# A new instruction list, and one accumulator moved, in the head of a fused state-space and feed-forward kernel

## The chip, the cores and the metric

The kernel runs on one core of a Trainium2 chip. The metric is the device time of one execution in microseconds (us). A core has a matrix engine (TensorE, PE in the profile; its weight loads are PEld), a vector engine (VectorE, DVE), a scalar engine (ScalarE, ACT), a general engine (GpSimd, POOL) and a fifth (SyncE, SP) that here only issues transfers. Each engine runs its own instructions strictly in the order in which they were written; engines wait for each other by semaphores. PE writes its results to PSUM, eight banks of 512 fp32 numbers per partition.

## The reference

Two layers. The first is a chunked state-space recurrence over 4 batches, 8 heads, 768 rows; the second is a feed-forward layer with a squared ReLU over the 3072 rows of 256 numbers that come out.

```python
log_a = np.log(np.clip(a, 1e-06, 1.0))
for c in range(nc):                                  # chunks of 32 rows
    cum = np.cumsum(la, axis=-1)
    L = np.exp(cum[:, :, :, None] - cum[:, :, None, :]) * causal
    M = np.einsum('bhin,bhjn->bhij', Cc, Bc) * L
    y_intra = np.einsum('bhij,bhjd->bhid', M, xc)
    y_inter = np.einsum('bhin,bhnd->bhid', Cc, state) * decay_to_i[:, :, :, None]
    y[:, :, sl] = y_intra + y_inter
    state = decay_full * state + np.sum(Bx, axis=2)  # Bx = B x, decayed to the chunk's end
...
h = np.maximum(x @ w_in, 0.0)
return h * h @ w_out
```

x has 32 numbers per head and row, B and C 16; w_in is 256 x 2048, w_out 2048 x 256.

## The kernel before

**Units and blocks.** The work is cut into 12 units of 256 rows of one batch with all 8 heads; unit k is batch k % 4 and third k // 4 of the rows. In the names, units and blocks count from 0, so "unit one" has the names that end in 0 (xs0, mts0, T0) and "unit two" those that end in 1. A unit's rows lie two to a partition (r = 0, 1), and its partitions in two halves of 64 (i = 0, 1), which are its two chunks: chunk 0 starts from the state before, chunk 1 from chunk 0's.

**The decay.** Instead of the decays between pairs of rows, the kernel uses the running product P of `a` within a chunk: C is multiplied by P and x by 1/P. `ac` clamps `a` (L538), `sk` is the scan that makes the running product (L470), `sp` and `p` bring it to rows on partitions by fp32 matmuls against an identity (`prep_p`, L454) and form chunk totals (L528, L549); copies out of PSUM make P_sb and Ptot (`ps`, `to`; `p` also copies), `iv` takes reciprocals (Pinv, L558), `fq` and `pq` make Pquad. The first 64 rows of `a` serve units 0 to 3 (`fa`, `ac0`, `sk0`, PSUM bank 4), the other 128 rows all later units (`la`, `ac1`, `sk1`, `pp1`, `p2`).

**A unit's steps**, in the order of its data: load B, C, x (`ldB`, `ldC`, `ldx`); C P and B to bf16 side by side in jt (`pc` L159, `pb` L167 and L171), x / P in xs (`px` L179); transposes on PE (`tr` L197, for unit 0 in the parts `trC` and `trB`) and their copies to bct (`tc`, `tcC`, `tcB`, L210 and L212); scores into banks 0 to 3, one for each pair of heads (`mt` L222); the causal mask, either directly (`mk`, DVE, L231) or by a score copy on ACT (`sc` L236) and a product on POOL or DVE (`ms` L240); state sums B'x (`u`, 16 matmuls, helper line L247); intra products (`in`; `ina` and `inb` are the halves that use the first and last two masks), the carry from the state (`ca`); copies T of the result (`t`, L210, L212, L284) and us of the state sums (`us`, L298). Sd is the state spread over four heads' blocks (`sf` straight from PSUM on DVE, L345; later `z`, L317 and L322, and `s` on POOL, L333). u, the intra products and the carry of a unit share a pair of banks; each engine's access to a bank waits for another engine's earlier one, whichever columns they use.

**The feed-forward layer.** Block k is unit k's 256 rows. For each of 8 groups f of 256 hidden features, `a0` to `l7` are the first layer's four matmuls of 256 columns (L405, bank by bank), with the ReLU on ACT into hb (L410); `qa0` and so on is the square on DVE (L416); `A0` to `L7` are the second layer's four matmuls (L432, accumulated in bank 6 or 7). The weights come in four loads each, issued by POOL (`wi` L140, `wo` L144).

**The order.** The kernel schedules by hand: the string ORDER lists every step, and each engine gets its instructions in the order of the list. A suffix `:a`, `:v`, `:p`, `:s` names the engine (ACT, DVE, POOL, SP). `id12:128` is twelve filler matmuls of 128 columns on constants (L477), which compute nothing that is used and keep PE running. `gB3` and `afC2` hold back the loads that follow by a small write or read on POOL.

Of the kernel before, what the change touches and what calls it, by code (L numbers as in the profile page):

```python
# [30 lines left out]
def kernel(  # L31
# [13 lines left out]
    nc = tc.nc  # L45
# [3 lines left out]
        fa1:a jz0:v ef jz1:p id12:128 ti fa0:s la0:s id15:128 pi eb ldB0:s ac0:v ldC0:a sk0 ku sp la1:a pbh0:p hd  # L49
        id1:256 pc0:v pbl0:v mb:a id7:128 trC0 ps iv:8:16 tcC0:1:a tcC0:0:v trB0 la2:s tcB0:2:v pk id4:128 iv1:0:8  # L50
        id2:256 ldx0:s mt0 wi0 la3:s px0:v ldC1:s ac1:p su id8:128 ldB1:s wi1 ldx1:s u0:67 mk0 mk0 mk0 pc1:p sc0
        pb1:a tr1 to id5:256 tc1:1:a tc1:0:v jz2:a ms0:p sk1 fq sf0 wo0 wi2 px1:p mt1 ina0 inb0 ca0 mk1 mk1 t0:aa
        sc1 us0 pp1:a mk1 a0 ldC2:s a1 u1 ina1 ms1:v pc2 inb1 p2 sf1 ca1 t1:va us1 a3 qa1 ldB2:s qa0 wo1 wi3 a2
        wo2 b0 qa3 qb0 b1 qb1 fr b2 b3 A0 A1 B0 pb2:p B1 tr2 zb0 qb3 b4 a4 iv:32:64 zb1 tc2:1:v qa2 tc2:0:v b5 sb1
        sb0 qb4 ldx2:s a5 qb2 qa4 mt2 gB3 sc2 ldB3:s ldC3:s B3 iv:16:32 px2 mk2 sc2 A3 ms2:v A2 mk2 qa5 a6 b6
        ms2:p B2 a7 qb5 pb3:a qa6 b7 A5 u2 ina2 ldx3:s inb2 sf2 wo3 pc3 px3 ld4 A4 tr3 ca2 tc3:1:v t2:aa B4 us2 B5
        tc3:0:v u3:45 pc4 mt3 us3 sc3 c5 qb7 qb6 mk3 za3 pb4 ld5 c3 qa7 c4 qc5 c0 tr4 qc3 px4 pb5 sa3 c1 c6 ld6
        qc4 pc5 tr5 qc0 A6 px5 pq A7 wm c2 B6 c7 C0 ms3:v mk3 qc6 mk3 qc7 afC2 pc6 pb6 B7 C3 C6 C4 qc1 bk rg4 C1
        qc2 d1 d0 za4 sa4 mk4 mk4 d3 mk4 C5 d4 qd0 d2 mk4 px6 C2 C7 ld7 zb4 qd1 sb4 qd2 qd3 zb3 rg5 sb3 D0 tr6 mk5
        za5 zb5 sa5 sb5 D1 iv:64:96 mk5 d5 qd4 D2 pb7 d6 qd5 d7 qd6 D3 zb2 e0 qd7 mk5 e1 qe0 sb2 D4 mk5 D5 ld8 pc7  # L60
        e2 qe1 D6 e3 qe2 px7 D7 rg6 e4 qe3 za6 sa6 tr7 zb6 mk6 e5 qe4 sb6 e6 qe5 e7 qe6 mk6 E0 E1 E2 E3 ld9 px8
        mk6 f0 qe7 E4 f1 qf0 pc8 E5 pb8 E6 mk6 f2 qf1 f3 qf2 E7 rg7 mk7 F0 f4 qf3 za7 tr8 F1 F2 f5 qf4 f6 qf5 f7
# [713 lines left out]
```

## Time and profile before

| what | us |
|---|---|
| median of 3 runs | 117.34 |
| the 3 runs | 117.34, 117.55, 115.72 |
| the profiled execution, its own time | 116.09 |
| its span, first to last instruction | 114.4 |
| mean granted clock of PE | 0.985 |
| PE, ACT, DVE, POOL busy | 108.4, 77.4, 84.4, 52.2 |

The rows that are shown below come from four views of that execution. A row of the timeline has the start in us, the busy time in us, the engine, the line of the kernel, the operation, output <- inputs, the shapes, how many were merged (x), and in brackets how long the engine was idle before it and what ended that. A row of the chain of waits has start, duration and what the chain went through. A row of the windows has the stretch, its length, the busy time and number of instructions of an engine, PE's granted clock, the share of the DMA engines and GB/s. A row of DMA issues has what is loaded, the queue, the size and the median time from issue to landing. Durations of PE overlap, as matmuls are pipelined.

### The profile page before, as it was taken

The page shows a single profiled execution, that of the slowest core. Times are in us where ns is not written, and L with a number is a line of the kernel's source. Part 1 is how long each engine was busy: PE and PEld are TensorE (multiplying, and loading weights), DVE is VectorE, ACT ScalarE, POOL GpSimd, SP SyncE. Part 2 cuts the span into 40 slices and gives each one's busy share as a digit, 9 for nine tenths or more (in the row PEclk, how much of TensorE's full clock was granted, in tenths as well). Part 3 has the DMA queues.
Part 4 walks back from the last instruction along what each step waited for, and adds up shares of the span by engine and source line. Part 5 has one row for each costly group of instructions (what it writes and reads, how often), then busy time and mean ns, then how long its engine had stood idle before and what let it go on. Part 6 is the DMA issues. An engine that isn't in the chain of part 4 may idle for free.

```text
span 114.4 us, 4062 instructions
## 1 busy us (share of the span) xinstructions
PE 108.4 (95%) x1658; PEld 96.5 (84%) x1658; DVE 84.4 (74%) x185; ACT 77.4 (68%) x158; POOL 52.2 (46%) x98
## 2 busy tenths in 40 slices
PE   7967899999999999999999999999999999999990
PEld 7845499898898889989989989989889899899980
DVE  2697566998899799989965989659578388345430
ACT  1744777677794785686587687786777776966840
POOL 7699950499298946659402769047020020000000
PEclk9999599999999999999999999999999999999999
DMA  2999999099998908988628538350051020020202
GB/s 40 198 196 193 217 196 188 10 183 169 189 163 140 317 10 181 215 192 164 131 80 158 112 113 149 87 145 19 6 141 22 6 95 0 14 83 0 92 6 92
DMA packets 47827, 13.47 MB, mean 118 GB/s; under 512 B 44288, under 2 KB 45888, under 8 KB 47808
## 3 DMA queue, kind: packets, MB, share of 16 engines
q1 hardware_dynamic: 44864, 10.88, 45.9%
q0 software_dynamic: 1664, 2.10, 11.4%
q10 hardware_dynamic: 1280, 0.23, 1.0%
q8 instruction: 13, 0.21, 0.7%
q14 instruction: 6, 0.05, 0.1%
HBM read 10.58 MB, written 3.15 MB: 120 GB/s over the span
## 4 chain that ended last, share of the span: by engine, by line
PE 87%; POOL 3%; DMA 3%; SPq 2%; issue 1%; ACT 1%; DVE 0%; ACTq 0%
PE pp L405 38%; PE pp L432 37%; PE pp L247 7%; PE pp L222 3%; DMA a_nat<-in_a_dram 3%; POOL mts L240 1%; SPq L565 1%; SPq L126 1%; POOL jt L159 1%; POOL w_in_b L140 1%; PE pp L197 1%; ACT T L210 1%; DVE Sd L345 0%; POOL a_cl L538 0%; SPq L116 0%
## 5 line engine op out<-in xcount | busy, mean ns | idle before, releaser
L410 ACT ACTIVATE hb<-pp 128x512 bf16<-128x512 f32 x96 | 54.6, 603 | 22.5 <-PE pp L405 21.4
L416 DVE TENSOR_TENSOR h<-hb 128x512 bf16<-128x512 bf16 x96 | 46.0, 498 | 12.1 <-ACT hb L410 11.8
L405 PE MATMUL pp<-T,w_in_b 128*128 128x256 bf16 x384 | 54.2, 276 | 0.5 <-ACT T L210 0.5
L432 PE MATMUL pp<-w_out_b,h 128*128 128x256 bf16 (+1 forms) x400 | 53.8, 268 | 0.0
L405 PEld LDWEIGHTS <-w_in_b 128*128 128x128 bf16 x384 | 41.8, 114 | 3.1 <-issue 1.8
L432 PEld LDWEIGHTS <-h 128*128 128x128 bf16 x400 | 37.7, 98 | 4.3 <-issue 0.6
L231 DVE TENSOR_TENSOR mts<-pp,mask 128x512 bf16<-128x512 f32 x43 | 28.5, 678 | 0.9 <-PE pp L222 0.9
L333 POOL TENSOR_TENSOR Sd<-z,Pquad 128x256 bf16<-128x256 f32 x16 | 10.6, 666 | 33.9 <-DVE z L317 24.0
L179 POOL TENSOR_TENSOR xs<-x_nat,Pinv 128x256 bf16<-128x256 f32 (+1 forms) x19 | 14.7, 788 | 3.8 <-DMA x_nat<-in_x_dram 2.4
L159 POOL TENSOR_TENSOR jt<-C_nat,P_sb 128x128 bf16<-128x128 f32 x22 | 9.5, 451 | 0.0
L317 DVE SCALAR_TENSOR_TENSOR z<-z,Ptot,us 128x64 f32<-128x64 f32 x8 | 2.4, 296 | 6.6 <-ACT us L301 5.5
L439 ACT COPY osb<-pp 128x512 f32<-128x512 f32 x11 | 6.4, 583 | 0.4 <-PE pp L432 0.4
L247 PE MATMUL pp<-mts,xs 64*32 64x128 bf16 x384 | 6.1, 226 | 0.5 <-DVE Sd L345 0.5
L477 PE MATMUL pp<-const-bfloat16-1.0 128*128 128x128 bf16 (+1 forms) x54 | 5.7, 275 | 0.8 <-PEq L760 0.8
L477 PEld LDWEIGHTS <-const-bfloat16-1.0 128*128 128x128 bf16 x54 | 4.6, 124 | 0.9 <-issue 0.8
L284 ACT CAST T<-pp 128x512 bf16<-128x512 f32 x7 | 4.1, 586 | 1.8 <-PE pp L247 1.5
L247 PEld LDWEIGHTS <-xs 64*32 64x32 bf16 x384 | 4.4, 94 | 0.8 <-issue 0.7
L222 PE MATMUL pp<-bct 32*64 32x256 bf16 x192 | 5.1, 280 | 0.0
L167 POOL CAST jt<-B_nat 128x256 bf16<-128x256 f32 x9 | 4.3, 473 | 1.1 <-DMA B_nat<-in_B_dram 1.1
L247 PE MATMUL pp<-bct,Sd 128*128 128x128 bf16 x40 | 4.3, 223 | 0.0
L210 ACT CAST T<-pp 128x256 bf16<-128x256 f32 x9 | 3.1, 376 | 1.5 <-PE pp L247 1.2
L197 PE MATMUL pp<-eye_b,jt 128*128 128x128 bf16 x24 | 2.5, 221 | 1.2 <-ACT Ptot L531 0.7
(67 smaller groups left out, 57.6 us busy)
## 6 DMA issues: line engine op xcount, KB each, us to landing
x_nat<-in_x_dram SPq DMA_DIRECT2D x12, 256.0 KB, 4.0
out_dram<-osb SPq DMA_DIRECT2D x11, 256.0 KB, 2.2
B_nat<-in_B_dram SPq DMA_DIRECT2D x12, 128.0 KB, 3.2
C_nat<-in_C_dram SPq DMA_DIRECT2D x11, 128.0 KB, 3.3
w_in_b<-in_moe_w_in_dram POOLq DMA_DIRECT2D x4, 256.0 KB, 5.9
w_out_b<-in_moe_w_out_dram POOLq DMA_DIRECT2D x4, 256.0 KB, 5.1
C_nat<-in_C_dram ACTq DMA_DIRECT2D x1, 128.0 KB, 2.5
bct<-jt SPq DMA_TRANSPOSE x8, 2.9
```

The lines of the kernel that those rows point to most:

```text
L159: eng.tensor_tensor(out=_fap(jt[k % 3], 128 + 144 * g, [[384, 2], [32, 4], [1, 16]]), in0=_fap(loaded[k]["C"], 128 * g, [[16, 2], [32, 4], ...
L179: eng.tensor_tensor(out=_fap(xs, 256 * r, [[256, 2 // n], [32, 8], [1, 32]]), in0=_fap(loaded[k]["x"], 32 * r, [[32, 2 // n], [64, 8], [1, ...
L222: nc.tensor.matmul(pp[64 * u:64 * u + 64, q, r * 256:r * 256 + 256], bct[32 * q:32 * q + 32, r, 0, u * 64:u * 64 + 64], _fap(bct[32 * q:32 ...
L231: nc.vector.tensor_tensor(out=live[k]["mts"][:, q].rearrange("p r g i -> p (r g i)"), in0=pp[:, q, :], in1=mask, op=ALU.mult)
L247: nc.tensor.matmul(dst, w, v, start=bool(need), stop=False, skip_group_check=True, **({} if pos is None else {"tile_position": pos}))
L333: nc.gpsimd.tensor_tensor(out=_fap(S_d, 0, [[128, 2], [32, 4], [1, 32]]), in0=_fap(z, 0, [[32, 2], [0, 4], [1, 32]]), in1=_fap(Pquad, 4 * ...
L405: nc.tensor.matmul(pp[:, h, i * 256:(i + 1) * 256], _fap(w, g * w.shape[2] + (o // 2) * 512 + 2 * (o % 2) + i, [[4, 128]]), T[blk][:, g].r ...
L410: nc.scalar.activation(out=hb.rearrange("p i t -> p (i t)"), in_=pp[:, h, :], func=AF.Relu)
L416: nc.vector.tensor_tensor(out=h2, in0=hb, in1=hb, op=ALU.mult)
L432: nc.tensor.matmul(dst, h2[:, i, r * 128:(r + 1) * 128], w_out_b[gi][:, 2 * o + i, c0:c1], start=first, stop=(fp == 7 and i == 1), skip_gr ...
L439: nc.scalar.copy(out=osb, in_=pp[:, 6 if blk == 1 else 7, :])
L477: nc.tensor.matmul(pp[:, h, 0:int(cols)], ones_b[:, 0:128], ones_b[:, 0:int(cols)] if dep is None else dep, start=True, stop=True, skip_gr ...
```

## The change

The head of ORDER is listed anew, up to the first steps of block 3; from `tr6` on the list is the same. Three definitions change with it. `u1:4` puts the state sums of chunk 0 of unit two (k = 1) into bank 4, columns 256 to 319, instead of the bank that its intra products use; us1 and Sd read them there. `p2` now only runs the fp32 products of the late rows of `a`, and its bank stays taken; the copies of Ptot and P_sb are the new step `pd2`. The mask copy moves from ACT to DVE (`mb:v`), the zeroing of jt0 from DVE to ACT and of jt2 from ACT to DVE (`jz0:a`, `jz2:v`), the first half of unit 0's B from DVE to POOL (`pbl0:p`), the second B copy of bct from DVE to ACT. On POOL the first weight issue (`wi0`) now stands ahead of the two B copies; on DVE the scan of the late rows (`sk1`) stands ahead of xs0 and of unit 0's masks; on ACT `pp1` and `ps` stand between the copies of bct0 and the score copy. On SP x of unit 0 is issued after the last two loads of `a` instead of between them. `ina0` and `inb0` come ahead of `mt1`, `tr2` and `mt2` ahead of the first `a4`. The fillers are 66 instead of 54.

```diff
     ORDER = """
-        fa1:a jz0:v ef jz1:p id12:128 ti fa0:s la0:s id15:128 pi eb ldB0:s ac0:v ldC0:a sk0 ku sp la1:a pbh0:p hd
-        id1:256 pc0:v pbl0:v mb:a id7:128 trC0 ps iv:8:16 tcC0:1:a tcC0:0:v trB0 la2:s tcB0:2:v pk id4:128 iv1:0:8
-        id2:256 ldx0:s mt0 wi0 la3:s px0:v ldC1:s ac1:p su id8:128 ldB1:s wi1 ldx1:s u0:67 mk0 mk0 mk0 pc1:p sc0
-        pb1:a tr1 to id5:256 tc1:1:a tc1:0:v jz2:a ms0:p sk1 fq sf0 wo0 wi2 px1:p mt1 ina0 inb0 ca0 mk1 mk1 t0:aa
-        sc1 us0 pp1:a mk1 a0 ldC2:s a1 u1 ina1 ms1:v pc2 inb1 p2 sf1 ca1 t1:va us1 a3 qa1 ldB2:s qa0 wo1 wi3 a2
-        wo2 b0 qa3 qb0 b1 qb1 fr b2 b3 A0 A1 B0 pb2:p B1 tr2 zb0 qb3 b4 a4 iv:32:64 zb1 tc2:1:v qa2 tc2:0:v b5 sb1
-        sb0 qb4 ldx2:s a5 qb2 qa4 mt2 gB3 sc2 ldB3:s ldC3:s B3 iv:16:32 px2 mk2 sc2 A3 ms2:v A2 mk2 qa5 a6 b6
...
+        fa0:s ku fa1:a ac0:v ldC0:a ef sk0 la1:a hd ti jz0:a pi jz1:p id25:128 la0:s pk jz2:v mb:v ldB0:s eb sp
+        iv1:0:8 wm pc0:v wi0 la2:s pbl0:p id1:512 pbh0:p id6:128 la3:s trC0 tcC0:0:a trB0 ac1:p tcB0:2:a ldx0:s
+        tcC0:1:v sk1 ldC1:s id6:128 ldB1:s mt0 pp1:a px0:v mk0 mk0 ps su u0:67 mk0 id8:128 sc0 id3:256 to pb1:a
+        ldx1:s id3:128 wi1 pc1:p tr1 ina0 ms0:p fq tc1:1:v inb0 ldC2:s iv:8:16 ldB2:s wo0 sf0 tc1:0:a px1:p wi2
+        mt1 mk1 mk1 id4:128 ca0 mk1 wo1 id1:128 t0:aa sc1 id9:128 us0 a0 ms1:v a1 u1:4 p2 ina1 sf1 inb1 zb0 ca1
+        t1:aa qa0 us1 wi3 pc2 a2 pd2 qa2 a3 qa3 qa1 pb2:a b0 ldx2:s b1 fr b3 b2 qb0 tr2 tc2:0:v tc2:1:v A0 A1 qb1
+        B0 qb3 iv:16:32 mt2 wo2 qb2 mk2 px2 pq gB3 B1 a5 a4 b4 ldB3:s sb0 b5 mk2 mk2 ldC3:s B3 qa4 A3 zb1 B2 mk2
...
-    def ph_u(k, h, begun):
+    def ph_u(k, h, begun, own=False):
         v, last = live[k], UNITS[k][1] == 2
         v["h"] = h
+        v["uat"] = [(4, 128 * (k + 1)) if own and i == 0 else (h[i], 256) for i in range(2)]
         for r in range(2):
             for i in range(2 - last):
                 for q in range(4):
-                    mm(begun, i, [q], pp[32 * q:32 * q + 32, h[i], 256:320],
+                    at, c = v["uat"][i]
+                    mm(set() if r == 0 and own and i == 0 else {(0, q)} if own and i == 0 else begun, i, [q], pp[32 * q:32 * q + 32, at, c:c + 64],
...
             nc.tensor.matmul(pp[:, h, 128:144], spread, pick_p[1], start=True, stop=True, skip_group_check=True)
+            busy.add(h)
+            second["h"] = h
+
+        second = {}
+
+        def second_out():
+            h = second["h"]
+            busy.discard(h)
             A.copy(out=Ptot[:, 8:24], in_=pp[:, h, 128:144])
             A.copy(out=P_sb[:, :, 32:96], in_=_fap(pp, h * 512, [[64, 2], [1, 64]]))
...
         def first_u(k, hs=None):
             v = live[k]
-            v["h"] = tuple(int(c) for c in hs) if hs else pair()
+            own = hs == "4"
+            v["h"] = ((6, 7) if k == 0 else pair()) if own else tuple(int(c) for c in hs) if hs else pair()
```

More of the change, by code (lines that the diff above doesn't have):

```diff
@@ L295, in ph_uc @@
         us = spool.tile([128, 2, 64], FP32, tag="us", name=f"us{k}", bufs=8)
-        h = v["h"]
-        if h[1] == h[0] + 1 and not last:
-            nc.scalar.copy(out=us, in_=_fap(pp, h[0] * 512 + 256, [[512, 2], [1, 64]]))
+        at = [512 * h + c for h, c in v["uat"]]
+        if not last and (at[1] - at[0] == 512 or v["uat"][0][0] == 4 and v["uat"][0][1] != 256):
+            nc.scalar.copy(out=us, in_=_fap(pp, at[0], [[at[1] - at[0], 2], [1, 64]]))
         else:
             for i in range(2 - last):
-                nc.scalar.copy(out=us[:, i], in_=pp[:, h[i], 256:320])
+                nc.scalar.copy(out=us[:, i], in_=_fap(pp, at[i], [[1, 64]]))
         v["us"] = us
```

36 lines of the change are left out of this document (18 added, 18 removed).

## The prediction

> **What bounds the kernel now.** I read the page first, then the chain of waits from the start to 45 us, then the timeline of the first 20 us engine by engine, and the busy time and clock in windows of 3.41 us, the length of the stretch at half clock.
>
> ```profile
> span 114.4 us, 4062 instructions
> ...
> PE 108.4 (95%) x1658; PEld 96.5 (84%) x1658; DVE 84.4 (74%) x185; ACT 77.4 (68%) x158; POOL 52.2 (46%) x98
> ...
> PEclk9999599999999999999999999999999999999999
> ```
>
> PE is busy for 95% of the span, so the end is fixed by two things: the matmuls that must be run, and the time at which PE gets into the dense stream of feed-forward matmuls. The fifth slice shows a clock of one half. The chain shows what stands before the stream:
>
> ```profile
> 3.26 2.92 DMA a_nat<-in_a_dram
> ...
> 6.27 0.41 POOL a_cl L538
> ...
> 7.37 0.73 POOL w_in_b L140
> ...
> 8.94 1.10 POOL mts L240
> 10.05 0.33 POOL Pquad L534
> ...
> 10.40 0.43 DVE Sd L345
> ...
> 11.67 0.64 ACT T L210 x2
> ...
> 12.35 1.87 PE pp L405 x8
> 14.22 0.60 PE pp L247 x42
> ...
> 15.66 2.66 PE pp L405 x24
> ...
> 29.27 0.28 ACT us L298
> ```
>
> The last load of `a` releases POOL; POOL's queue (clamp, a weight issue, C of unit two, the mask product, Pquad) releases the first state Sd, the carry, the copies of T, and then a0 and a1, the first eight feed-forward matmuls, at 12.35. From 15.66 the chain is PE without a break, but for the copy of us3 at 29.27. A later start of this stream is paid in full.
>
> ```profile
> 4.10:7.51 3.41, 3.28 (x70) 1.00 1.00 193
> 7.51:10.92 3.41, 1.88 (x31) 1.00 1.21 201
> 10.92:14.33 3.41, 2.94 (x62) 0.50 1.17 211
> ```
>
> Columns: window, its length, PE busy and matmuls, granted clock, DMA share, GB/s. After a window in which PE was busy 1.88 of 3.41 us (55%), the next has half the clock; after one of 86% it is whole again. So a0 and a1 took 1.87 us, against 8/24 of 2.66, 0.89, later.
>
> **The head, step by step.** The list moves most of the first 150 instructions, so I place the new order with the durations of the old one.
>
> ```profile
> 4.00 0.19 POOL L481 TENSOR_SCALAR_AFFINE_SELECT quad<-quad 128x4 f32<-128x4 f32 x1
> 4.71 0.29 POOL L171 CAST jt<-B_nat 128x128 bf16<-128x128 f32 x1 [0.52 <-DVE jt L159]
> 4.97 0.21 ACT L700 COPY P_sb<-pp 128x64 f32<-128x64 f32 x1 [0.70 <-DVE jt L159]
> 5.22 0.25 DVE L558 RECIPROCAL Pinv<-P_sb 128x16 f32<-128x16 f32 x1
> 5.26 0.93 POOL L140 DMA_DIRECT2D w_in_b<-in_moe_w_in_dram  x1 [0.26 <-issue]
> 5.89 0.42 PE L222 MATMUL pp<-bct 32*64 32x256 bf16 x16
> 6.12 0.69 DVE L179 TENSOR_TENSOR xs<-x_nat,Pinv 128x512 bf16<-128x512 f32 x1
> 6.27 1.04 POOL L538 TENSOR_SCALAR a_cl<-a_nat 128x128 f32<-128x128 f32 x1
> 6.46 0.59 ACT L236 CAST sc<-pp 128x512 bf16<-128x512 f32 x1 [0.38 <-PE pp L222]
> 6.73 1.88 DVE L231 TENSOR_TENSOR mts<-pp,mask 128x512 bf16<-128x512 f32 x3
> 8.18 0.77 POOL L159 TENSOR_TENSOR jt<-C_nat,P_sb 128x128 bf16<-128x128 f32 x2
> 9.34 0.36 DVE L212 COPY bct<-pp 128x384 bf16<-128x384 bf16 x1 [0.73 <-PE pp L197]
> 9.61 0.73 DVE L470 TENSOR_TENSOR_SCAN cp<-a_cl,const-float32-0.0 128x128 f32<-128x128 f32 x1
> 12.82 0.34 ACT L542 ACTIVATE pick_p<-pick,cp 128x16 f32<-128x16 f32 x1
> ```
>
> POOL's constants end at 4.19 in either order. Then the first weight issue now stands ahead of the B copies: 4.19 + 0.26 + 0.93 = 5.38; two B copies of 0.29, one of them DVE's before, end at 5.96. The last load of `a` is issued one place earlier, as x of unit one now follows it; at the old 2.92 us it lands about 5.7. So the clamp starts at 5.97 instead of 6.27. Its length is uncertain: the chain gives it 0.41, the timeline 1.04. I carry both ends: 6.38 or 7.01.
>
> The scores of unit one come later: from the old B copy's end (5.00) to the scores (5.89) were 0.89 us, so 6.85 now, over by 7.27. This costs nothing by itself, since the scan of the late rows stands ahead of x and of the masks on DVE, and waits for the clamp. Queued behind that wait on DVE are xs0, three mask products and the copy for unit two's scores; PE (u0, the intra products, mt1) waits for these. Scan 0.73: 7.16 or 7.79 with 0.05 for the hand-over. xs0 0.69: 7.87 or 8.5, against 6.81 before. Masks 1.88: 9.77 or 10.4, against 8.61. Copy of bct1 0.36, reciprocal 0.25, Sd 0.43: 10.85 or 11.5. DVE replaces POOL as what ends last: the other feeder runs pick_p 0.34, P_sb 0.21 and score copy 0.59 on ACT to 8.35 or 9.0, C of unit two 0.77 and mask 1.10 and Pquad 0.33 on POOL to 10.0 or 10.65, and is early.
>
> What the change gains here is behind Sd. Before, Sd's end (10.83) to a0 (12.35) took 1.52 us, with all the intra products and both copies of T inside. Now the intra products run in halves before it, and only the carry (some 0.3) and two overlapped T copies, half of the 0.64 being exposed, remain: I take 0.85, for a0 at 11.7 or 12.35, a gain of 0.65 or nothing. The fillers are under these waits and cost nothing: PE has nothing else there.
>
> **From a0 to the dense stream.** Here two things go.
>
> ```profile
> 12.82 0.52 DVE L240 TENSOR_TENSOR mts<-sc,mask 128x512 bf16<-128x512 bf16 x1 [0.20 <-ACT sc L236]
> 14.85 0.42 DVE L345 TENSOR_TENSOR Sd<-pp,Pquad 128x256 bf16<-128x256 f32 x1 [1.50 <-PE pp L247]
> 7.57 0.41 ACT L167 CAST jt<-B_nat 128x256 bf16<-128x256 f32 x1 [0.53 <-DMA B_nat<-in_B_dram]
> 16.22 3.09 ACT L410 ACTIVATE hb<-pp 128x512 bf16<-128x512 f32 x6
> 20.00:25.00 5.00, 4.90 (x12) 1.00 0.42 71
> ```
>
> Sd of unit two waited 1.50 us for PE, because the intra products wrote the bank that holds its sums; with the sums in bank 4 it waits for u1 alone. And if PE keeps its whole clock, a0 and a1 take 0.89. PE's side: a0 + 0.89 + (15.66 - 14.22 =) 1.44 gives 14.0 or 14.7. DVE's side: Sd + masks 1.88 + 0.52 + Sd 0.42 + the carry gives 14.0 or 14.65. They agree: the stream starts 1.66 or 0.96 us earlier than 15.66. I take the middle, 1.3, as nothing tells the two clamp lengths apart. The fp32 products are on PE either way; their copies, moved behind an eviction, cost ACT the same and are 0.3 us of cover.
>
> Some of it is given back. ACT has, behind the T copies (about 14.5), us1, Ptot and P_sb, B of unit three (0.41) and evictions at 3.09/6 = 0.515 each; tr2, now ahead of the first second-layer products, waits for that B copy until about 16.95, where PE would arrive at 14.0 + 2.66 = 16.66. And DVE, busy 4.90 us of the 5 from 20 to 25 (last row), has the squares and the masks of unit three in the same stretch; a wait for a mask can take some 0.5. Bounds: zero if DVE catches up as it did, 1.0 if both are paid. I take 0.4, below the middle, since the shift also moves DVE's inputs forward. The us3 copy (0.28 and hand-overs) is now behind B5: 0.3 gained.
>
> The weights are no bound:
>
> ```profile
> w_in_b<-in_moe_w_in_dram POOLq DMA_DIRECT2D x4, 256.0 KB, 5.9
> ```
>
> The first lands about 4.5 + 5.9 = 10.4, before 11.7. The rest, after 30 us, has the same instructions in the same order.
>
> **Sum.** -1.3 + 0.4 - 0.3 = -1.2: a span of 113.2. The profiled execution's own time was 116.09 for 114.4, so 1.69 more: 114.9; rounding kept, 114.84, I say 114.8. Own range: 116.09 - 1.66 - 0.3 = 114.1 to 116.09 - 0.96 + 1.0 - 0.3 = 115.8. The profiled time is 1.25 below the median of the three runs (117.34, from 115.72 to 117.55); if that scatter is the clock's, it goes with it. Two per cent of 117.34, about what a measurement of this kernel can tell from no change, is 2.35: the marks are 114.99 and 119.69.
>
> Two rules beside the rows. First, the clock: the 55% window is the row above, and its longest wait of PE is this one, 0.65:
>
> ```profile
> 8.03 0.23 PE L197 MATMUL pp<-eye_b,jt 128*128 128x128 bf16 x1 [0.65 <-ACT Ptot L531]
> ```
>
> The Trainium skill (TensorE: Matmul & The Clock Gate, Why this matters for your kernels) asks only for no idle gap of over about 3 us; by that rule neither kernel would lose its clock, and the clock term of this sum would be zero, but this trace disagrees: the clock fell after waits of 0.65 at most. Second, the scan: 0.73 us on 128 rows stood beside POOL's mask product. The Trainium skill (GPSIMD Engine Reference, 1. Specifications) says that GpSimd shares its SBUF interfaces with VectorE and contends with instructions of two SBUF inputs; by it the scan, now beside a weight issue, could be shorter, which no row here separates from the larger tile.
>
> **Rivals.**
>
> *The clock falls all the same.* Between 7.27 and xs0 (7.87 or 8.5) PE is idle, 0.36 or 0.99 us of the window that ends at 10.92, so at most 89% or 71% busy, where 55% lost the clock and 86% kept it. If lost, the stretch from a0 to 14.33 runs at half: 2.0 to 2.6 us lose 1.0 to 1.3, ACT is no longer late, and 0.3 stays: 116.09 - 1.3 + 1.15 - 0.3 = 115.6.
>
> *ACT and DVE take it all.* The dense stream starts early and is held at tr2, mt2 and the masks of unit three, with DVE at 98% there: 116.09 - 0.96 + 1.0 = 116.1, the 0.3 of us3 swallowed too: no change.
>
> *The scan holds DVE for a late load.* Speaks for it: DVE's queue stands behind one small load, and the first weight transfer now starts before that load must land.
>
> ```profile
> C_nat<-in_C_dram SPq DMA_DIRECT2D x1, 128.0 KB, 5.8
> ```
>
> This C load, issued at 5.93 beside the first weights, took 5.8 us. If the `a` load of 2.79 is slowed as much, it lands at 8.6, 2.6 after the clamp's place. All behind it moves by 2.6 from the late end (a0 at 14.95), and PE, idle till 11, loses its clock for one whole window, half of 3.41: 1.7. With 0.7 given back and the 0.3 of us3: 116.09 - 0.96 + 2.6 + 1.7 + 0.7 - 0.3 = 119.8. It is slower than the median from a slip of about 0.1 us with that window lost, and over the mark from 2.5. Against it: 16 KB, and issued before the weights.
>
> **Chances.** Forecast 0.56, of which 0.40 lies under 114.99; clock falls 0.20; ACT and DVE take it 0.10; the scan held 0.14. So faster 0.40, same 0.46, slower 0.14. The range goes from 113.6 (both low ends, and 0.5 for steps priced too long) to 118.0 (the clock's case, on the scatter of 1.25 above, and a slip below 1).
>
> **What would show it.** In the profile of the changed kernel: the clamp at about 6 and the scan right behind it; xs0 ending at 7.9 to 8.5 and the masks at 9.8 to 10.4; a0 at 11.7 to 12.35; Sd of unit two with no wait for intra products; no half in the clock line after 10 us; 24 feed-forward matmuls from 14.0 to 14.7. Wrong if the scan waits past 7.1, if a half clock stands after 11 us, or if PE has breaks of over 1 us between 16 and 24.

## The result, and the profile after

The changed kernel took 118.88 us in the median of 4 runs (117.76 to 119.50), the kernel before, beside it, 117.08 us (115.72 to 117.55). The ratio is 1.0282, with a 95% interval from 1.0215 to 1.0349: slower, where 114.8 was forecast. This ratio, like those below, is of fast runs alone, those within 1.5% of the fastest of their kernel; the two medians would give 1.015.

| | before | after |
|---|---|---|
| profiled execution, its own time, us | 116.09 | 119.50 |
| its span, us | 114.4 | 117.8 |
| mean granted clock of PE | 0.985 | 0.971 |
| first weight issue on POOL, start, us | 5.26 | 4.43 |
| B of unit two: copy on ACT, start, us | 7.57 | 11.19 |
| stream of 24 feed-forward matmuls, start, us | 15.50 | 18.77 |

(The 15.66 of the prediction is the same start in the chain of waits, which counts a matmul from the end of the one before; from here on I use the timeline's.) The page of the changed kernel:

```profile
span 117.8 us, 4074 instructions
...
PE 110.3 (94%) x1670; PEld 98.0 (83%) x1670; DVE 81.5 (69%) x185; ACT 76.2 (65%) x157; POOL 50.1 (43%) x98
...
PEclk9998559999999999999999999999999999999999
```

DVE, ACT and POOL have less to do than before. The clock line has a half in two slices, the fifth and the sixth, instead of in the fifth alone. The chain of waits of the changed kernel says what came first:

```profile
4.38 6.73 DMA B_nat<-in_B_dram
...
11.19 0.41 ACT jt L167
...
11.65 0.82 PE pp L197 x6
...
15.47 1.71 PE pp L407 x8
...
18.93 2.62 PE pp L407 x24
```

Before, the chain went from a load of `a` through POOL to the first state. Now it goes from SP's load of B of unit two, which takes 6.73 us to land, over its copy on ACT, to the transposes of unit two on PE. That load was issued at 4.35 before, 0.03 us earlier, and landed in 3.2 us, so that its copy started at 7.57. The timelines of POOL, DVE, ACT and PE give the rest of the head:

```profile
4.43 0.93 POOL L140 DMA_DIRECT2D w_in_b<-in_moe_w_in_dram  x1
6.00 0.65 POOL L540 TENSOR_SCALAR a_cl<-a_nat 128x128 f32<-128x128 f32 x1
...
6.68 0.42 DVE L472 TENSOR_TENSOR_SCAN cp<-a_cl,const-float32-0.0 128x128 f32<-128x128 f32 x1 [0.94 <-POOL a_cl L540]
7.02 0.67 DVE L179 TENSOR_TENSOR xs<-x_nat,Pinv 128x512 bf16<-128x512 f32 x1
7.61 1.88 DVE L231 TENSOR_TENSOR mts<-pp,mask 128x512 bf16<-128x512 f32 x3
...
11.19 0.41 ACT L167 CAST jt<-B_nat 128x256 bf16<-128x256 f32 x1 [3.00 <-DMA B_nat<-in_B_dram]
...
11.65 0.82 PE L197 MATMUL pp<-eye_b,jt 128*128 128x128 bf16 x6 [2.39 <-ACT jt L167]
...
18.77 2.78 PE L407 MATMUL pp<-T,w_in_b 128*128 128x256 bf16 x24
```

Clamp, scan, scaled x and masks of unit one run as forecast or a little earlier (masks done at 9.49). Then ACT stands 3.00 us for the load and PE 2.39 us for ACT, and intra products, scores and everything else are queued behind these transposes. The windows of the changed kernel show what the gap does to the clock:

```profile
7.51:10.92 3.41, 1.65 (x32) 1.00 1.13 186
10.92:14.33 3.41, 2.68 (x62) 0.51 1.21 198
14.33:17.74 3.41, 3.41 (x43) 0.50 0.87 141
```

PE was busy 1.65 us of 3.41 (48%) in the first of these, and in the next two it had half its clock. The first of those two was itself busy for only 79%, at half clock.

### The profile page after: what moved, and what is told of

It reads as the page before. It is cut to its first block, busy times and chain, and to the rows that moved or that the text cites. A ratio compares the mean times of both kernels' runs of the same rounds, so it can differ in the third digit from the quotient of the medians.

```text
span 117.8 us, 4074 instructions
## 1 busy us (share of the span) xinstructions
PE 110.3 (94%) x1670; PEld 98.0 (83%) x1670; DVE 81.5 (69%) x185; ACT 76.2 (65%) x157; POOL 50.1 (43%) x98
## 4 chain that ended last, share of the span: by engine, by line
PE 87%; DMA 6%; SPq 3%; POOL 1%; ACT 1%; issue 1%; ACTq 0%
PE pp L407 37%; PE pp L434 35%; PE pp L247 7%; DMA B_nat<-in_B_dram 6%; PE pp L222 4%; PE pp L479 1%; SPq L126 1%; SPq L575 1%; PE pp L197 1%; POOL xs L179 1%; PE pp L456 0%; ACT jt L167 0%; SPq L116 0%; PE pp L551 0%; ACT osl L745 0%
## 5 line engine op out<-in xcount | busy, mean ns | idle before, releaser
L412 ACT ACTIVATE hb<-pp 128x512 bf16<-128x512 f32 x96 | 55.3, 604 | 24.2 <-PE pp L407 22.1
L418 DVE TENSOR_TENSOR h<-hb 128x512 bf16<-128x512 bf16 x96 | 44.0, 477 | 13.2 <-ACT hb L412 13.0
L231 DVE TENSOR_TENSOR mts<-pp,mask 128x512 bf16<-128x512 f32 x45 | 29.8, 680 | 1.2 <-PE pp L222 1.2
L479 PE MATMUL pp<-const-bfloat16-1.0 128*128 128x128 bf16 (+1 forms) x66 | 7.1, 279 | 0.8 <-PEq L771 0.8
L479 PEld LDWEIGHTS <-const-bfloat16-1.0 128*128 128x128 bf16 x66 | 5.8, 126 | 1.5 <-issue 1.2
L212 DVE COPY bct<-pp 128x384 bf16<-128x384 bf16 (+1 forms) x5 | 1.6, 341 | 4.9 <-PE pp L197 4.9
L197 PEld LDWEIGHTS <-jt 128*128 128x128 bf16 x24 | 1.8, 107 | 3.5 <-ACT jt L167 2.6
```

The source lines that it names most:

```text
L231: nc.vector.tensor_tensor(out=live[k]["mts"][:, q].rearrange("p r g i -> p (r g i)"), in0=pp[:, q, :], in1=mask, op=ALU.mult)
L412: nc.scalar.activation(out=hb.rearrange("p i t -> p (i t)"), in_=pp[:, h, :], func=AF.Relu)
L418: nc.vector.tensor_tensor(out=h2, in0=hb, in1=hb, op=ALU.mult)
L479: nc.tensor.matmul(pp[:, h, 0:int(cols)], ones_b[:, 0:128], ones_b[:, 0:int(cols)] if dep is None else dep, start=True, stop=True, skip_gr ...
```

## The experiments

Medians below stand beside the kernel before on the same chip: 115.50 us for e1 to e4 (19 runs), 115.50 for e5 to e7 (14), 115.23 for e8 to e10 (19), 115.29 for e11 and e12 (1), 116.75 for e13 to e16 (7), 115.23 for e17 and e18 (17). "Stream" is the start of the 24 feed-forward matmuls in the timeline of the profiled execution, "later loss" what PE then lost by waits or half clock behind that start, in the same profile. Where no interval stands, the record gives none.

| run | median us | ratio, 95% interval | span | clock | stream | later loss | span - stream - loss |
|---|---|---|---|---|---|---|---|
| before | 117.08 | | 114.4 | 0.985 | 15.50 | 0 | 98.9 |
| after | 118.88 | 1.0282 [1.0215, 1.0349] | 117.8 | 0.971 | 18.77 | 0.15 | 98.9 |
| e1 | 116.23 | 1.0047 [1.0003, 1.0091] | 114.8 | 1.000 | 16.00 | 0 | 98.8 |
| e2 | 120.18 | | 118.3 | 0.971 | 19.45 | 0 | 98.9 |
| e3 | 117.42 | | 114.0 | 1.000 | 15.14 | 0 | 98.9 |
| e4 | 116.65 | 1.0107 [1.0069, 1.0146] | 114.9 | 1.000 | 16.17 | 0 | 98.7 |
| e5 | 116.71 | 1.0124 [1.0057, 1.0191] | 113.9 | 1.000 | 14.28 | 0.81 | 98.8 |
| e6 | 115.41 | 0.9986 [0.9941, 1.0030] | 113.0 | 1.000 | 14.22 | 0 | 98.8 |
| e7 | 116.47 | 1.0120 [1.0060, 1.0179] | 116.8 | 0.985 | 16.32 | 1.67 | 98.8 |
| e8 | 115.48 | 1.0011 [0.9961, 1.0060] | 115.6 | 0.970 | 16.44 | 0.32 | 98.8 |
| e9 | 116.66 | 1.0105 [1.0005, 1.0206] | 115.1 | 0.985 | 16.36 | 0 | 98.7 |
| e10 | 115.87 | 1.0040 [0.9996, 1.0084] | 114.4 | 1.000 | 15.22 | 0 | 99.2 |
| e11 | 115.84 (1 run) | | 114.1 | 0.985 | 15.37 | 0 | 98.7 |
| e12 | 118.08 (1 run) | | 116.4 | 0.971 | 16.92 | 0.57 | 98.9 |
| e13 | 116.82 (1 run) | | 115.1 | 1.000 | 14.63 | 1.70 | 98.8 |
| e14 | 116.36 (1 run) | | 114.6 | 1.000 | 14.89 | 0.81 | 98.9 |
| e15 | 116.68 (1 run) | | 115.0 | 1.000 | 14.62 | 1.48 | 98.9 |
| e16 | 119.08 | | 115.5 | 0.985 | 16.49 | 0 | 99.0 |
| e17 | 116.70 | 1.0123 [1.0080, 1.0165] | 116.6 | 0.985 | 16.16 | 1.67 | 98.8 |
| e18 | 116.26 | 1.0048 [1.0003, 1.0092] | 113.9 | 0.993 | 14.12 | 1.0 | 98.8 |

The later loss is a wait of PE that the profile names, or what the 24 matmuls took over 2.78 us (2.82 in the kernel before) where half clock reached into them, or for e18 the time by which the end of the program, behind PE's last matmul, was longer than in the others (3.97 us against 2.93 to 3.01). The last column makes the table readable: the program behind the start of the stream takes 98.7 to 99.2 us in all of them, so a kernel's span is its stream's start, plus what it loses later, plus about 98.8.

**The weights and the load beside them.** e1 undoes one step of the change, e2 does that step alone in the kernel before.

```diff
 e1, in the changed list
-        iv1:0:8 wm pc0:v wi0 la2:s pbl0:p id1:512 pbh0:p id6:128 la3:s
+        iv1:0:8 wm pc0:v la2:s pbl0:p id1:512 pbh0:p wi0 id6:128 la3:s
 e2, in the list before: wi0 (behind mt0) moved ahead of pbh0
```

> The changed list with one step moved: the first weight issue goes back behind the two B copies on POOL, so that it starts at about 5.3 instead of 4.43. Theory W (the earlier weight transfer takes the DMA engines from the B load of unit two): that load, issued at 4.4 as before, lands near 7.6 to 8.3 instead of 11.1, PE's wait of 2.4 us before the transposes of unit two goes, the half clock after 11 us goes or is one window, and the time falls by 3 to 4.5 us from 118.9, to 114.5 to 116. Theory X (the loads are late because x of unit one is issued behind the last loads of a): the B load still lands after 10 and the time stays within 1 us of 118.9. Theory C (the list is slow through ACT and DVE behind 12 us anyway): the B load lands early but the time stays above 117.

> The kernel before with the reverse move alone: the first weight issue stands ahead of the B copy on POOL, at about 4.4 instead of 5.26. Theory W: the B load of unit two lands at 9 to 11 instead of 7.6, and the time rises from 117.1 by 1.5 to 4 us. Theory X: x of unit one is still issued between the loads of a, so the B load lands by 8.3 and the time stays within 1 us of 117.1.

In e1, the timelines of POOL, ACT and PE:

```profile
5.45 0.93 POOL L140 DMA_DIRECT2D w_in_b<-in_moe_w_in_dram  x1
...
8.54 0.40 ACT L167 CAST jt<-B_nat 128x256 bf16<-128x256 f32 x1
...
15.55 0.40 PE L247 MATMUL pp<-mts,xs 64*32 64x128 bf16 x14 [1.42 <-issue]
...
16.00 2.78 PE L407 MATMUL pp<-T,w_in_b 128*128 128x256 bf16 x24
```

With the first weight issue 1.02 us later, the copy of B on ACT has no wait any more (8.54, in ACT's own order), the clock is whole throughout, and the time falls from 1.0282 to 1.0047 of the kernel before: of the change's loss, 2.35 points of 2.82, or some 2.7 us, hang on this one step. In e2, the same views:

```profile
4.12 0.93 POOL L140 DMA_DIRECT2D w_in_b<-in_moe_w_in_dram  x1
...
11.64 0.40 ACT L167 CAST jt<-B_nat 128x256 bf16<-128x256 f32 x1 [4.11 <-DMA B_nat<-in_B_dram]
...
12.10 0.51 PE L197 MATMUL pp<-eye_b,jt 128*128 128x128 bf16 x6 [4.23 <-ACT Ptot L531]
```

The step alone makes the kernel before slower than the changed one: 120.18 us (118.24 to 120.78) against 115.50 (114.90 to 118.70). Its load of B took 7.26 us in the chain. (The releaser that the last row names for PE is the next entry of ACT's queue, which stood behind that copy and so behind the load.) The kernel before is 0.9 us away from this loss: its weights are issued 0.91 us behind B, and B lands in 3.2 us.

Is it B that is delicate, or anything beside that transfer? e16 keeps the weights early and moves only the load of B ahead of them.

```diff
-        ... ldB0:s eb sp
+        ... ldB0:s ldB1:s eb sp
-        tcC0:1:v sk1 ldC1:s id6:128 ldB1:s mt0
+        tcC0:1:v sk1 ldC1:s id6:128 mt0
```

> The changed kernel with nothing moved but the load of B of unit two, on SP from behind C of unit two to right behind B of unit one; the first weight issue stays ahead of the copies of B. Theory W (what the change lost is this load, slowed by the weights that now start ahead of it): it lands before 7, its copy on ACT no longer waits, TensorE has no gap of over 1.5 us after 9, and the time is 115.5 to 116.7, as in e1. Rival: the weights slow whatever is in flight beside them, then the late rows of a (issued some 0.5 us later here) or x of unit one land late in its place, and the time stays above 117.5.

The rival was right, with a load that I had not named. B is in time (its copy at 8.00, no wait), and now C of unit two is late; the chain of waits and the timeline of POOL:

```profile
4.65 5.65 DMA C_nat<-in_C_dram
...
10.48 0.75 POOL L159 TENSOR_TENSOR jt<-C_nat,P_sb 128x128 bf16<-128x128 f32 x2 [3.07 <-DMA C_nat<-in_C_dram]
```

The median is 119.08 us (117.17 to 120.56) against 116.75 (114.70 to 118.03). So it is not a property of B. Over all the profiles, by the time from a load's issue to its landing:

| profile | load | weights issued, relative to it, us | to landing, us |
|---|---|---|---|
| before, e8, e10, e12 | B of unit two | 0.9 to 1.3 behind | 3.2, 3.4, 3.2, 3.6 |
| e1, e5, e6, e15 | B of unit two | 1.0 to 1.1 behind | 3.6, 3.5, 3.7, 4.1 |
| e7, e9, e11, e13 | B of unit two | 0.9 to 1.1 behind | 3.8, 3.2, 3.8, 3.8 |
| e14, e17, e18 | B of unit two | 0.8 to 1.0 behind | 3.5, 4.5, 3.5 |
| after, e4 | B of unit two | 0.05 behind, 0.04 ahead | 6.7, 6.5 |
| e2 | B of unit two | 0.24 ahead | 7.3 |
| e16 | C of unit two | 0.31 ahead | 5.7 |
| e3 (below) | B of unit two | 0.08 behind | 3.9 |
| e2 | C of unit two | 0.23 behind | 3.9 |
| e16 | x of unit one (256 KB) | 0.15 behind | 3.3 |

B of unit two in e3 stands against it, and so do the last two rows: a load can be issued close to the weights and be spared. The packets of the DMA queues show more. The first packets of the weights run about 2 us after their issue: none until 6.4 us in the changed kernel and in e3, none until 7 us in the kernel before. From 7 to 9 us, first in the changed kernel, then in the kernel before (queue, packets, MB, share of the 16 DMA engines' time; q0 is POOL's queue, q1 SP's):

```profile
q0 software_dynamic: 210, 0.21, 71.2%
q1 hardware_dynamic: 448, 0.06, 26.2%
...
q0 software_dynamic: 182, 0.19, 56.5%
q1 hardware_dynamic: 897, 0.22, 51.8%
```

So what is late is whatever SP's queue has not yet moved when the weights' packets begin. In the kernel before, B had landed by 7.55; in the changed kernel it had not, and SP's queue moved 0.06 MB in those 2 us instead of 0.22. e3 has x of unit one issued 0.47 us earlier than the changed kernel, and its SP queue moved 0.22 MB from 4 to 5 us where the changed kernel's moved 0.07, so that less of B was left. This fits that profile of e3; no run tests it.

What of the loss is the wait, and what the clock? e4 leaves the wait and keeps PE busy through it with more fillers.

```diff
-        ldx1:s id3:128 wi1 pc1:p tr1
+        ldx1:s id45:128 wi1 pc1:p tr1
```

> The changed list with 42 more filler matmuls of 128 columns, some 2.3 us at full clock, where PE waits for the B load of unit two; nothing else moves. It tells the wait from the clock. If the clock is most of the loss: the half clock from 11 to 17.7 goes, a0 still starts near 15 or before, and the time falls by 1.5 to 2.5 us from 118.9, to about 116.5 to 117.4. If the wait alone is the loss: the clock stays whole but the time falls by under 0.7.

ACT and PE in e4:

```profile
10.95 0.41 ACT L167 CAST jt<-B_nat 128x256 bf16<-128x256 f32 x1 [2.84 <-DMA B_nat<-in_B_dram]
...
16.17 2.78 PE L407 MATMUL pp<-T,w_in_b 128*128 128x256 bf16 x24
```

B is as late as in the changed kernel, 2.84 us of wait against 3.00, but the clock is 1.000 and the stream starts at 16.17 instead of 18.77: of these 2.60 us, 0.24 is B's earlier landing and some 2.4 the clock's. By the ratios it is 1.75 points of 2.82.

**What is left of the forecast.** With the weights moved back, PE should have reached the stream at 14.0 to 14.7. e1's profile has 16.00, because PE stood 1.42 us in the middle of the intra products of unit two (row above), with masks, state and scaled x long done. e3 keeps the weights early and puts the load of x of unit one back between the late rows of `a`; e5 has e1's list with the same filler columns in 39 fewer matmuls (1631 instead of 1670; its expectation has 42, a miscount); e6 is e5 and e3's move together; e7 is e5 with the change's bank undone.

```diff
 e3
-        pbh0:p id6:128 la3:s trC0 tcC0:0:a trB0 ac1:p tcB0:2:a ldx0:s
+        pbh0:p id6:128 ldx0:s la3:s trC0 tcC0:0:a trB0 ac1:p tcB0:2:a
 e5, on e1 (and likewise for the other groups of fillers)
-        ... jz1:p id25:128 la0:s
+        ... jz1:p id6:512 id1:128 la0:s
 e7, on e5
-        a1 u1:4 p2 ina1
+        a1 u1 p2 ina1
```

> The changed list with x of unit one issued again between the last two loads of a on SP, 0.5 us earlier; the weight issue stays early. Theory X: the B load of unit two lands by 8.3 and the time falls by 3 us or more from 118.9. Theory W: it still lands after 9.5 and the time stays within 1 us of 118.9.

> The changed kernel with the first weight issue behind the copies of B (as in e1_wi0_behind_b) and the same columns of filler matmuls in fewer, wider instructions: 42 matmuls fewer ahead of the intra products of unit two. Theory F (in e1 TensorE stood 1.42 us in the middle of the intra products of unit two, with masks and states long done, because its own instructions came late: the page's row 'q8 instruction: 13 packets' is a queue that brings them in blocks): the 33rd to 42nd matmul after that place now lies where the block ends, so the stall of 1.42 us leaves 14.13 and is gone or shows, shorter, inside the stream of weight products that follows; stream from 14.6 to 15.4 instead of 16.0; time 114.6 to 115.6, that is 0.6 to 1.4 us under e1. Rival G (the stall belongs to something that those products wait for, a buffer or a semaphore that the profile does not name): same stall at the same instruction, time as e1, 116.0 to 116.5.

> e5_wide_fillers with the load of x of unit one issued between the late rows of a, as in before. Theory F with x no bound in e5: same as e5, within 0.5 us. If x of unit one sets the scaled inputs of unit one (they started at 7.02 in after), the products of unit one start up to 0.4 us earlier and the time falls to 114.2 to 115.2. If the late rows of a, now behind x, become the bound for the second clamp and scan, 0.3 to 1 us slower than e5.

> e5_wide_fillers with unit two's first state sums back in the bank of its output (the change's own bank undone, all else kept). If that bank is worth what I put on it (the 0.30 us copy of the states and the scaled state S may be read while the intra products of unit two are still being written), the scaled state waits for the end of those products and TensorE stands 0.5 to 0.9 us ahead of the carry product: time 0.4 to 1.0 us over e5. If nothing waits there, within 0.3 us of e5.

e3's four runs went from 115.71 to 118.55 us, with clocks from 1.000 to 0.971, and its profile, the fastest of them, is the one in which B was spared. With the weights early it can go either way; what decides between e3's own runs is not shown, as only one of them has a profile. e5, PE:

```profile
13.76 0.46 PE L247 MATMUL pp<-mts,xs 64*32 64x128 bf16 x32
...
14.28 2.78 PE L407 MATMUL pp<-T,w_in_b 128*128 128x256 bf16 x24
```

All 32 intra products run in one piece and the stream starts at 14.28: the forecast's 14.0 to 14.7. e6 has 14.22 and a span of 113.0, also the forecast's (113.2). But by its runs e6 is no faster than the kernel before (0.9986), and e5 is slower. In e7 the profiled execution has a wait that belongs to the undone bank:

```profile
15.86 0.40 PE L247 MATMUL pp<-mts,xs 64*32 64x128 bf16 x16 [0.51 <-DVE Sd L347]
```

PE waits 0.51 us for the state product in the middle of the intra products, as expected for a shared bank, yet e7's runs are as long as e5's (1.0120 and 1.0124). The bank is worth 0.5 us at its place in this profile. At the end nothing of it shows, but intervals of 0.6% to either side, some 0.7 us, are too wide to rule 0.5 us out.

e10 asks the same of all that the change is named by: the kernel before, its head and its weights where they were, with only these edits.

```diff
-        to id5:256 tc1:1:a tc1:0:v jz2:a ms0:p sk1 fq sf0 wo0 wi2 px1:p mt1 ina0 inb0 ca0
+        to id5:256 ina0 tc1:1:a tc1:0:v jz2:a ms0:p sk1 fq sf0 inb0 wo0 wi2 px1:p mt1 ca0
-        a1 u1 ina1 ms1:v pc2 inb1 p2 sf1 ca1
+        a1 u1:4 p2 ina1 ms1:v pc2 sf1 inb1 ca1
```

> The kernel before with only the three edits that the change is named by: intra products of unit one in halves ahead of unit two's scores, first state sums of unit two in bank 4, and the fp32 products split from their copies; the head as before, the first weight issue too. If these are worth what the prediction put on them (Sd of unit two no longer waits 1.50 us for TensorE, and the intra products leave the stretch between Sd and a0), 0.3 to 1.0 us under the kernel before. If the masks of unit two on DVE hold the end instead, the same within 0.3. If the scores of unit two behind the second half of the intra products delay those masks, 0.3 to 0.8 us slower.

Its median is 115.87 against 115.23, ratio 1.0040 [0.9996, 1.0084]: nothing gained. DVE in e10:

```profile
11.89 1.89 DVE L231 TENSOR_TENSOR mts<-pp,mask 128x512 bf16<-128x512 f32 x3 [0.86 <-PE pp L222]
...
14.12 0.42 DVE L347 TENSOR_TENSOR Sd<-pp,Pquad 128x256 bf16<-128x256 f32 x1
```

The state product of unit two no longer waits for PE (before: 1.50 us), as forecast. But the masks of unit two start at 11.89 instead of 10.74, after 0.86 us of wait for the scores, which now stand behind the second half of the intra products; three masks, a fourth and the state product follow each other on DVE to 14.54. One wait was taken away and another put in, and the stream starts at 15.22.

e9 tries the scan's place, which the prediction had as what ends last in the head: e6 with the scan behind the masks of unit one, the scaled x ahead of it.

```diff
-        tcC0:1:v sk1 ldC1:s ... mt0 pp1:a px0:v mk0 mk0 ps su u0:67 mk0 ... to pb1:a
+        tcC0:1:v px0:v ldC1:s ... mt0 ps mk0 mk0 su u0:67 mk0 sk1 ... to pb1:a pp1:a
```

> e6_wide_x0 with the scan of the late rows of a moved behind the three masks of unit one, the scaled x of unit one ahead of it, and on ACT the copy of P ahead of the second pick. In e6 the chain runs clamp (6.48, 0.66), scan (7.16), pick, copy of P (7.92), chunk sums on TensorE at 8.08 after 1.44 us of idle time, and from there TensorE without a break to the end. If the scan's place ahead of the masks costs what I put on it (masks 1.1 us later than before), the sums come at 6.7 to 7.3, the stream of 24 products at 13.5 to 13.9 instead of 14.22, time 0.3 to 0.7 us under e6 (114.7 to 115.1). If x of unit one lands as late as the scan ends (7.5), or DVE's masks of unit two hold the end, the same as e6 within 0.3.

The ratio is 1.0105 [1.0005, 1.0206]: no gain, and probably a loss. The chunk sums come at 6.56 instead of 8.08, as expected. But at its new place the scan runs beside POOL's products for unit two, and it takes 1.81 us instead of 0.42:

```profile
8.56 1.81 DVE L472 TENSOR_TENSOR_SCAN cp<-a_cl,const-float32-0.0 128x128 f32<-128x128 f32 x1
...
10.40 0.31 ACT L544 ACTIVATE pick_p<-pick,cp 128x16 f32<-128x16 f32 x1 [2.38 <-DVE cp L472]
```

ACT waits 2.38 us for it, and the copy of unit two's transposes, next on ACT, is late for PE by 0.60 us. Ahead of that PE waits 0.37 us for C of unit two and 0.37 for the mask product on POOL, and the clock is lost for one window. So the longer scan, which the expectation did not have, takes back much of what the new place gains; that is read from these rows, and no run tests it.

**What the kernel before does at full clock.** The stream of e5 and e6 starts 1.2 to 1.3 us ahead of the 15.50 of the profile that I predicted from, and the kernels are still no faster. e8 and e12 are the kernel before itself.

> The kernel before itself, for a profile of it in which TensorE keeps its whole clock. Of its runs beside e1 most had a clock of 1.0 and a span of 113.2 to 113.6, those with 0.985 one of 114.5 to 115.0, with 0.97 of 115.5 or more; the profiled run that the prediction read had 0.985 and 114.4. If that run's half clock at a0 and a1 is what separates it, the stream of 24 weight products starts at 14.4 to 14.9 here instead of 15.66, so that the 1.3 us of my forecast was in part a gain over a lost clock which the kernel before mostly does not lose, and what is left for the change is 0.3 to 0.5 us. If the half clock is lost elsewhere or the stream starts at 15.5 or later at full clock, the forecast's reference was right.

> The kernel before once more, for a profile at full clock. In every profile so far the span is the start of the stream of 24 weight products plus 98.7 to 99.6 us (before 15.50 and 114.4, e1 16.00 and 114.8, e5 14.28 and 113.9, e6 14.22 and 113.0, e9 16.36 and 115.1). At full clock, span 113.0 to 113.6, the stream of the kernel before then starts at 14.1 to 14.8: as early as the best version of the changed list. If it starts at 15.3 or later with such a span, the rule does not hold and the kernel before saves time behind the head.

Neither gave the profile I wanted: their profiled executions had clocks of 0.970 and 0.971. e12's stream:

```profile
16.92 3.39 PE L405 MATMUL pp<-T,w_in_b 128*128 128x256 bf16 x24
```

It starts at 16.92, and its 24 matmuls take 3.39 us instead of 2.82, as the half clock reaches into them. But 7 of e8's 11 runs had a clock of 0.998 to 1.000 and spans of 113.1 to 113.9. By the last column of the table a span of 113.3 means a stream at 14.5 (an estimate; no profile shows it). So the kernel before, when it keeps its clock, enters the stream as early as the best of the changed lists, and the 15.50 of its profile (clock 0.985) was about 1.0 us of lost clock.

**The break in the intra products.** I thought the 1.42 us of e1 were PE's own instructions coming late, at a fixed place of its program, as the page has a queue of 13 packets that only brings instructions. Then more or fewer filler matmuls ahead of it must move the break by as many places.

```diff
 e11, e13, e14, each on e1 (e15 is e1 unchanged)
-        id25:128
+        id37:88          e11
+        id13:246         e13
+        id33:97          e14
```

> e1_wi0_behind_b with the first 25 fillers of 128 columns cut into 37 of 88 columns: twelve matmuls more ahead of everything else, the same columns, no other edit. Theory F (the stall of e1 is TensorE's own instructions coming late, at a fixed place of its program): the break moves by twelve matmuls in the list, from after the 18th of the 32 intra products of unit two to after the 6th, with 0.5 to 1.7 us, and TensorE reaches it some 0.2 us earlier. Rival G (something that those products read or write is late): the break stays after the 18th, or is gone. If there is no break at all, neither is told apart, as e1's own runs at full clock had spans from 113.3 to 114.8.

> e1_wi0_behind_b with the first 25 fillers of 128 columns as 13 of 246: twelve matmuls fewer, the same columns. Theory F (TensorE's own instructions come late, at a fixed place of its program): the break, if there is one, stands twelve matmuls later in the list than in e1, after the 30th of the 32 intra products of unit two, and it is shorter by the time that these take (about 0.3 us): 0.4 to 1.1 us. Rival G (something those products read or write is late): after the 18th, or none.

> e1_wi0_behind_b with the first 25 fillers as 33 of 97 columns: eight matmuls more. Theory F: the break, if there is one, after the 10th of the 32 intra products. Rival G: after the 18th, or none.

> e1_wi0_behind_b unchanged, one more look. Theory F: a break after the 18th of the 32 intra products of unit two, of 0.5 to 1.5 us, or none if the block of instructions happens to land early. Rival G: a break at the same place, or at another step that reads what is late.

None of the four has a break. It stood in e1 (1.42 us) and e3 (0.77), and in e17 below again, each time after the 18th of the 32 products, and these three have the same number of instructions ahead of it; no list with another number has shown one of that size (after, e16 and e15, with the same number, do not show it either). That fits the guess, but a break at a shifted place was never seen. The cause stays open.

**Where an early stream loses again.** e15 starts its stream at 14.62, 1.38 us ahead of e1, and its span is 0.2 us longer. Its chain of waits, and its timelines of POOL and PE:

```profile
22.10 6.41 DMA x_nat<-in_x_dram
```

```profile
22.79 0.61 POOL L144 DMA_DIRECT2D w_out_b<-in_moe_w_out_dram  x1
...
28.64 1.29 POOL L179 TENSOR_TENSOR xs<-x_nat,Pinv 128x512 bf16<-128x512 f32 x1 [3.08 <-DMA x_nat<-in_x_dram]
...
29.99 0.25 PE L247 MATMUL pp<-xs,jt 64*32 64x64 bf16 x16 [1.48 <-POOL xs L179]
```

PE stands 1.48 us for the scaled x of unit four: that load takes 6.41 us, and a weight load was issued 0.69 us behind it. The weight load cannot be the whole cause, as in e6 one was issued 0.71 us behind this load, which landed in 3.84. The same wait is in e5 (0.81), e13 (1.70) and e14 (0.81), and not in e6, where the scaled x could start at 25.66. e17 puts x first among the loads of unit four in e1's list, e18 does so in e6's.

```diff
-        px2 pq gB3 B1 a5 a4 b4 ldB3:s sb0 ... wo3 ldx3:s sf2
+        px2 pq gx3 B1 a5 a4 b4 ldx3:s ldB3:s sb0 ... wo3 sf2
```

> e1_wi0_behind_b with the loads of unit four in another order: x first, behind the same hold on POOL, then B and C (before: B, C, x). In e15, the second look at e1, the stream started at 14.62, but the span was 115.0: TensorE stood 1.48 us at 29.99 for the scaled x of unit four, whose load was issued at 22.10 and landed 6.4 us later; in e13, e14 and e5 the same wait took 1.70, 0.81 and 0.81. Theory X (what the earlier stream gains is given back there): x is issued 1.1 us earlier, the wait falls below 0.5, span 113.4 to 114.0, time 115.1 to 115.7, 0.6 to 1.3 under e15. Rival: B, now later, or the transfers together are what is late, and the wait moves to the transposes of unit four or stays: span 114.6 or more.

> e6_wide_x0, the best so far, with the same order of unit four's loads. e6's profile had no wait for the scaled x of unit four (its load landed 3.9 us after its issue), so by theory X the profile is as e6's, span 112.9 to 113.3, and only those of its runs that lost time there gain: a median of 114.8 to 115.4, at or up to 0.5 us under the kernel before. Rival: B of unit four becomes late: 0.3 to 1 us slower.

Both miss. e17 took 116.70 us (ratio 1.0123 [1.0080, 1.0165]); its profiled execution had the break again, and by it lost the clock, so that its stream was too late to meet that wait:

```profile
15.71 0.40 PE L247 MATMUL pp<-mts,xs 64*32 64x128 bf16 x14 [1.58 <-issue]
...
16.16 4.45 PE L407 MATMUL pp<-T,w_in_b 128*128 128x256 bf16 x24
```

e18, 116.26 us, 1.0048 [1.0003, 1.0092], has its stream at 14.12, no wait of PE behind it, and yet a span of 113.9. Its clock of 0.993 is not the reason: the half clock begins at 112.29, when PE has been done since 109.9, as early as in e6 (110.1). What is longer is the issue of the last outputs on SP, first in e18, then in e6:

```profile
109.68 2.00 SPq L746 DMA_DIRECT2D out_dram<-osl  x2
...
109.85 0.81 SPq L746 DMA_DIRECT2D out_dram<-osl  x2
```

Why it takes longer is not shown. Its other runs lie from 115.06 up. So the wait for x of unit four is shown in four profiles, and that taking it away helps is not. No version is faster than the kernel before; e6 is as fast.

## Why the prediction was wrong, step by step

- *POOL, clamp and scan.* Right. The first weight issue ended at 5.36 (forecast 5.38), the clamp started at 6.00 (5.97) and took 0.65, between the two ends of 0.41 and 1.04. The scan took 0.42 instead of 0.73 and masks ended at 9.49 instead of 9.77. The shorter scan is what the Trainium skill (GPSIMD Engine Reference, 1. Specifications) would have: beside a POOL mask product it took 0.73, beside a weight issue 0.42, on the same 128 rows, so that the larger tile, which the prediction could not rule out, is not the reason.
- *"The weights are no bound."* This is the step that failed. I asked only when the first weights land (before 11.7), and priced the moved issue as 0.93 us of POOL's time. A moved DMA issue is also a moved transfer, and beside the transfer of 256 KB the landing of B of unit two went from 3.2 to 6.73 us. e1 and e2 show it from both sides, and e16 shows it with another load. The term was put at nothing although a row of the prediction has ACT waiting 0.53 us for this very load (7.57, B_nat): it had no slack to lose.
- *The third rival* had this mechanism, its model row (a C load of 5.8 us beside the weights) and the loss of the clock after it, at 119.8 us. It named the load of `a` that was issued 1.6 us ahead of the weights, which landed in time, and passed over the one issued 0.05 us ahead of them: the load that suffers is the one still on its way when the packets of the weights begin, not the one whose waiter comes first.
- *The clock.* The forecast had it kept, one rival had it lost for 1.15 us. It was lost for two windows, some 2.4 us (e4), through the wait for B. The Trainium skill (TensorE: Matmul & The Clock Gate, Why this matters for your kernels) asks for no idle gap of over about 3 us. PE's longest here was 2.39 us, so this trace again disagrees; busy shares of 48% (after) and 55% (before) in a window of 3.41 us lost the clock, and 70% (after, 2.37 of 3.41, from 4.10 to 7.51) kept it. But the share is no sharp rule in these traces: behind 2.25 of 3.41 (66%) the clock fell in e7 (at 16.70), and behind 2.19 (64%) it stayed whole in e2 (at 9.10). Nor does 86% always bring it back, as the prediction read it: in e2 another half followed it (at 15.92).
- *a0 to the dense stream.* Right once the weights are out of the way: the state product waits for no PE, and the stream starts at 14.28 (e5), 14.22 (e6), 14.62 (e15), where 14.0 to 14.7 was forecast.
- *The sum, -1.3.* Wrong in its reference. I subtracted from a profile that had itself lost half a clock window at a0 and a1. By the runs of e8 the kernel before mostly keeps its clock, and its span is then 113.1 to 113.9, where the forecast had 113.2 for the changed kernel. I had written that the scatter of the three runs goes with the clock, if it is the clock's, and not drawn the conclusion: the gain then is the same clock, counted for the change. (The terms add up to 114.89; the 114.84 does not come out of them, which changes nothing.)
- *The 0.3 of the us3 copy.* It does not show: from the start of the stream to the end, less the later loss, the kernel before takes 98.8 to 98.9 us and the changed lists 98.7 to 99.0.
- *The give-back of 0.4.* At a place that was not on my list. tr2, mt2 and the masks of unit three cost nothing in e5 or e15; x of unit four cost 0.81 to 1.70.

## What to carry to other kernels

A DMA issue that is moved is two moves: the issuing engine's time, and a transfer that now runs beside other loads. List the loads issued within a microsecond of its new place, those that will still be on their way when its packets begin, and who waits for each, before asking when the moved transfer itself lands. And before a gain is taken from one profile, compare its clock and span with the other runs of the same kernel: what that execution lost by chance is no gain of the change.

## What the runs showed of the hardware

The load of B of unit two (128 KB, from SP) took 3.2 to 4.5 us to land in the fifteen profiles in which a weight load of 256 KB was issued from POOL 0.8 to 1.3 us behind it. Issued within 0.24 us of the weights, it took 6.5 to 7.3 us in three profiles (after, e2, e4) and 3.9 in one (e3); C of unit two, issued 0.31 us behind them, took 5.7 (e16). The Trainium skill (DMA: Bandwidth & Descriptors, Queues, rings and completion order) says that each DMA engine takes the queues that it has work for in turn, packet by packet. The trace agrees so far that both queues move packets in the same 2 us, but not in equal parts: from 7 to 9 us in the changed kernel the weights' queue has 71% of the engines' time, and SP's 26%. What the section does not say, and the fifteen show, is that 0.8 us of distance is enough to be spared, or nearly so.

The scan of 128 rows took 0.41 to 0.43 us in the fifteen profiles in which no product of POOL ran beside it, and 0.73, 0.73, 0.73, 1.39 and 1.81 us in the five in which one did (before, e8, e10, e12, e9).

And PE stood three times 0.77 to 1.58 us at the same place of its program with nothing that the profile shows to wait for.
